# Turning stage one's result of batch 0 on VectorE, with the head of the kernel rearranged

## The chip, the cores and the metric

The kernel runs on one core of a Trainium2 chip. The metric is the device time of one execution in microseconds (us). TensorE is called PE, VectorE DVE, ScalarE ACT, GpSimd POOL and SyncE SP, as in the profile.

## What is computed

For each of 8 batches of 3072 rows by 256 columns, the real part of a two-dimensional Fourier transform; then, row by row, a maxout layer with three weight matrices and an output matrix:

```python
X = np.fft.fft(x, axis=1)
X = np.fft.fft(X, axis=2)
x = X.real.reshape(B * S, D)                 # B, S, D = 8, 3072, 256
h = np.maximum(np.maximum(x @ w1, x @ w2), x @ w3)   # 256 -> 768
out = h @ w_out                                       # 768 -> 256
```

## The kernel before, in words

The transform along the columns is folded into the weights: the matrices `md` and `nmd` hold its sines and cosines, and the products (L290 to L317) of them with w1, w2, w3 give the stationary operands `gE`, `gO` and `gD` of the main loop. The transform along the 3072 rows is split as 32 times 96 and done in two stages per batch.

- **Loading and mirroring.** POOL's queue loads x (L117), and a copy with reversed columns (`mirror`, L124) fills the lower 64 partitions: one copy at L129 and one of a single column at L131. For batch 0 both are on DVE, in four chunks (`FIRST`).
- **Stage one**, `Mix.s` (L365): seven matrix products per batch with the table `tab`; each result in PSUM is evicted to the tile `tb` (L372, L376), with partitions as frequency and the 49 positions s along the row.
- **The turn.** Stage two needs s on the partitions. `Mix.y` (L378) stores `tb` to a DRAM buffer `db` and `Mix.z` (L388) reads it back as `yb`. In batch 0 this is done in six stores and four reads on the queues of SP and ACT. `Mix.u`, `Mix.x0` and `Mix.c` compute one extra column of `yb` from the first column of x.
- **Stage two**, `Mix.k(which, g)` (L406): small products of `yb` with the tables `te_tab` and `to_tab` for one third g of the frequencies; evictions at L413 to `tE` and `tO`, the operands of the main loop. `Mix.end` (L423) does the middle frequency.
- **Tables.** `angle` (L263) reduces the angles in `kvec` with four DVE passes and `table` (L276) makes sines with three ACT passes. Thirds 0 and 1 are done ahead of the loop, the last third (columns 1024 to 1536) by entries of the plan in units 1 to 3.
- **Main loop** (L791 to L829): 18 units per batch, 144 in all. A unit forms two products per 128 hidden columns (`unit_plus`, L430; `unit_minus`, L440), ACT applies relu (`stmp`, L450), DVE takes the maximum into `hp` and `hm` (L451), and the output products (L460) of the previous block are woven in. `third` moves part of odd units to POOL.

The order of the work is written out by hand: engines take instructions in the order of the program, and a plan (L672 to L738) says behind which unit each piece of the next batch's transform is emitted: `ahead0` for batch 1 during batch 0, `ahead` for later ones. `warm_up` (L586) issues products of zeros that keep PE busy while it waits.

Of the head of the program, the order that the prediction follows is at L590 to L637: angles of two thirds on DVE, stage one in three groups with the stores between them, md_all and nmd_all, the first tables, the four reads, the second half of the weights only once a read has landed (L618, L597), four products with 384 columns each, then `m.k(0, 0)` and `m.k(1, 0)`, whose evictions the first unit of the loop waits for.

Of the kernel before, what the change touches and what calls it, by code (L numbers as in the profile page):

```python
# [9 lines left out]
FP32 = mybir.dt.float32  # L10
BF16 = mybir.dt.bfloat16
INT32 = mybir.dt.int32
AX = mybir.ActivationFunctionType
ALU = mybir.AluOpType
# [36 lines left out]
def kernel(  # L51
# [20 lines left out]
    KS = 2 * NS  # L72
# [8 lines left out]
    dbs = [d_pool.tile([NS, 4 * RI * 128], BF16, name=f"db{i}", tag=f"db{i}") for i in range(2)]  # L81
# [5 lines left out]
    tb = consts.tile([128, 25 * 128], BF16, tag="tb")  # L87
    tbv = tb.rearrange("p (s f) -> p s f", f=128)
    yb = consts.tile([128, 2 * RI * 128], BF16, tag="yb")
    x0s = consts.tile([128, RI], BF16, tag="x0s")  # L90
    x0u = consts.tile([128, KS + 1], BF16, tag="x0u")
    ybv = yb.rearrange("p (r e f) -> p r e f", e=2, f=128)
# [13 lines left out]
    gE = [consts.tile([128, DFF], BF16, name=f"gE{i}", tag=f"gE{i}") for i in range(2)]  # L106
    gO = [consts.tile([128, DFF], BF16, name=f"gO{i}", tag=f"gO{i}") for i in range(2)]
    gD = [consts.tile([128, DFF], BF16, name=f"gD{i}", tag=f"gD{i}") for i in range(2)]
# [15 lines left out]
    def mirror(b, s0, s1):  # L124

        t = xt[b % 2]
        fn = (nc.vector.tensor_copy, (nc.gpsimd.tensor_copy, nc.vector.tensor_copy)[s0 >= 25],
              nc.scalar.copy)[min(b, 2)]
        fn(out=t[64:128, s0:s1, 1:128], in_=t[0:64, s0:s1, 255:128:-1])  # L129
        if b < 2:  # L130
            fn(out=t[64:128, s0:s1, 0], in_=t[0:64, s0:s1, 128])  # L131
# [18 lines left out]
    ang_r = gen.tile([128, 4 * RI], FP32, tag="ang_r")  # L150
    iota(ang_r, [[0, 4], [1, RI]], base=1)
    iota(ang_r.rearrange("p (g r) -> p g r", r=RI)[:, :, 15:17], [[0, 4], [16, 2]])
# [9 lines left out]
    def load_w(jh, after=None):  # L162
        for wsrc, wdst in ((moe_w1, w1_bf), (moe_w2, w2_bf), (moe_w3, w3_bf)):
            ld = nc.gpsimd.dma_start(
                out=wdst.rearrange("p (fc j) -> p fc j", fc=2)[:, :, jh * 384:(jh + 1) * 384],
                in_=wsrc.rearrange("(fc p) j -> p fc j", fc=2)[:, :, jh * 384:(jh + 1) * 384])
            if after is not None:
                tc.add_manual_dep(ld.ins, after.ins.name, AFTER, reason="others first")

    load_w(0)  # L170
# [3 lines left out]
    for r in (0, 6, 11):  # L174
        n = {0: 6, 6: 5, 11: 4}[r]
        iota(kv[:, r:r + n, :], [[1, n], [32, 96]], base=r + 1)
    iota(kvec[:, 1408:1504].rearrange("p (r j) -> p r j", r=2), [[16, 2], [32, 48]])
# [3 lines left out]
    rows_f = gen.tile([128, 12 * B], FP32, tag="rows_f")  # L181
    iota(rows_f.rearrange("p (b t u) -> p b t u", t=4, u=3), [[S, B], [-4, 4], [-1025, 3]],
         base=S - 1, cm=-32)
    zero = gen.tile([128, 512], BF16, tag="zero")
    nc.vector.memset(zero, 0.0)
    for db in dbs:
        pads = db[:, 64 * 128:].rearrange("s (r c) -> s r c", c=256)
        nc.sync.dma_start(out=pads, in_=zero[0:NS].rearrange("p (r c) -> p r c", c=256))
# [5 lines left out]
    ang_o = gen.tile([128, 4 * RI], FP32, tag="ang_o")  # L194
    nc.vector.memset(ang_o, 0.0)
    nc.vector.memset(ang_o[:, 0:RI], 8.0)
    nc.vector.memset(ang_o[:, 3 * RI:4 * RI], 24.0)
# [3 lines left out]
    def scal(out, in0, s1, op0, s2=None, op1=None, eng=None):  # L201
# [3 lines left out]

    up, sidx, hflag, alpha, sig, sgm = (small(n) for n in
                                        ("up", "sidx", "hflag", "alpha", "sig", "sgm"))
    scal(up, pidx, 64.0, ALU.is_ge)
    nc.vector.scalar_tensor_tensor(out=sidx, in0=up, scalar=-64.0, in1=pidx,
                                   op0=ALU.mult, op1=ALU.add)  # L210
    scal(hflag, sidx, 32.0, ALU.is_ge)
    scal(alpha, sidx, -2.0, ALU.mult, 31.0, ALU.add)
    nc.vector.scalar_tensor_tensor(out=alpha, in0=alpha, scalar=hflag, in1=sidx,
                                   op0=ALU.mult, op1=ALU.add)
# [3 lines left out]
    ang_q = gen.tile([128, 4 * RI], FP32, tag="ang_q")  # L218
    nc.vector.scalar_tensor_tensor(out=ang_r, in0=ang_r, scalar=alpha, in1=ang_o,
                                   op0=ALU.mult, op1=ALU.add)  # L220
    _reduce(nc, ang_r, ang_r, ang_q, 32.0)
    nc.scalar.activation(out=ang_q, in_=ang_r, func=AX.Sin, scale=float(2.0 * math.pi / 32.0))
    nc.vector.tensor_copy(out=tab[:, 0:64:2], in_=ang_q[:, 0:32])
    scal(tab[:, 1:64:2], ang_q[:, 0:32], sig, ALU.mult)
    scal(tabx, ang_q[:, 2 * RI:4 * RI], sgm, ALU.mult)

    dve = nc.vector.tensor_copy
    half = gen.tile([128, 256], FP32, tag="half")
    nc.vector.memset(half[:, 0:128], 64.0)
    nc.vector.memset(half[:, 128:256], 0.0)  # L230

    vm = gen.tile([128, 512], FP32, tag="vm")
    qm = gen.tile([128, 512], FP32, tag="qm")
    pf = gen.tile([128, 2], FP32, tag="pf")
    par = gen.tile([128, 2], FP32, tag="par")
    for fc in range(2):
# [4 lines left out]
            in1=half.rearrange("p (k c) -> p k c", c=128), op0=ALU.mult, op1=ALU.add)  # L241
    mirror(0, *FIRST[0])
    _reduce(nc, vm, vm, qm, 256.0)
    mirror(0, *FIRST[1])
    mirror(0, *FIRST[2])
    scal(par[:, 1:2], pidx, 0.5, ALU.mult, -0.25, ALU.add)
    scal(par[:, 1:2], par[:, 1:2], ROUND, ALU.add)
    mirror(0, *FIRST[3])
    scal(par[:, 1:2], par[:, 1:2], -ROUND, ALU.add, -2.0, ALU.mult)
    nc.vector.tensor_tensor(out=par[:, 1:2], in0=par[:, 1:2], in1=pidx, op=ALU.add)  # L250
    scal(par[:, 1:2], par[:, 1:2], 64.0, ALU.mult)
    scal(par[:, 0:1], par[:, 1:2], -1.0, ALU.mult, 64.0, ALU.add)
    nc.vector.tensor_copy(out=vm.rearrange("p (fc k c) -> p fc k c", fc=2, k=2)[:, :, :, 0],
                          in_=par.unsqueeze(1).to_broadcast([128, 2, 2]))
    phi, s_of = small("phi"), small("s_of")
    scal(phi, par[:, 1:2], 12.0, ALU.mult, 768.0, ALU.add)
    scal(s_of, par[:, 1:2], -1.0 / 64.0, ALU.mult)
    nc.vector.tensor_tensor(out=s_of, in0=s_of, in1=pidx, op=ALU.add)
    scal(s_of, s_of, 0.5, ALU.mult)
    q = gen.tile([128, NHALF + 1], FP32, tag="q")  # L260
    step = float(2.0 * math.pi / 3072.0)

    def angle(part, c0=1024, c1=NHALF + 1):  # L263
        cs = slice(c0, c1)
        if part == 0:
            scal(kvec[:, cs], kvec[:, cs], s_of, ALU.mult, phi, ALU.add)
# [4 lines left out]

    def angles(c0, c1):
        for part in range(2):
            angle(part, c0, c1)
# [11 lines left out]
    def tables(c0, c1):  # L286
        for k in range(3):
            table(k, c0, c1)

    def product(i, half, jh, pool, tag):  # L290

        psg = pool.tile([128, 512], FP32, name="psg", tag=tag)
        hs = slice(half * 128, (half + 1) * 128)
        for k, (table, wt) in enumerate(((md, (w2_bf, w3_bf)[i]), (nmd, w1_bf))):
            for fc in range(2):
                nc.tensor.matmul(
                    psg[:, 0:384], table[fc][:, hs],
                    wt[:, fc * DFF + jh * 384: fc * DFF + jh * 384 + 384],
                    start=(k == 0 and fc == 0), stop=(k == 1 and fc == 1))
        return psg  # L300

    def keep_product(psg, i, half, jh, evict_e):

        cs = slice(jh * 384, (jh + 1) * 384)
        if half == 0:
            evict_e(out=gE[i][:, cs], in_=psg[:, 0:384])
        else:
            nc.scalar.copy(out=gO[i][:, cs], in_=psg[:, 0:384])
            nc.vector.tensor_scalar(out=gD[i][:, cs], in0=gO[i][:, cs], scalar1=dif,
                                    scalar2=None, op0=ALU.mult)  # L310
# [551 lines left out]
```

## Time and profile before

| what | us |
|---|---|
| runs shown | 400.01, 401.09, 401.16 (median 401.09) |
| the profiled execution's own time | 400.15 |
| its span, first to last instruction | 397.9 |
| PE busy | 382.8 (96%) |
| DVE busy | 317.6 (80%) |
| ACT busy | 259.6 (65%) |
| POOL busy | 324.6 (82%) |
| granted PE clock, mean | 0.989 of full |

The page of the profile shows the execution in 40 slices of 9.9 us; a digit is the busy share of an engine in tenths:

```
PE   7598999999999999999999999999999999999994
DVE  6977797877887887877887877887887887887982
ACT  2577689768856788568866788568766547544420
PEclk9799999999999999999999999999999999999999
```

PE is below nine tenths only in the first four slices and the last. The second slice, 10 to 20 us, is where PE is busy half the time and has a lower clock; all that the prediction works out lies there and in the two slices behind it.

### The profile page before, as it was taken

To read this page: it belongs to the slowest core of one execution; us is meant where nothing else is said; L and a number is where in the kernel's file an instruction comes from. 1 tells how busy PE (TensorE), PEld (TensorE's weight loads), DVE (VectorE), ACT (ScalarE), POOL (GpSimd) and SP (SyncE) were. 2 spreads that over 40 slices of the span, in tenths; PEclk is the share of its full clock that TensorE was granted. 3 is DMA by queue.
4 is the path that set the end of the run, shared out by engine and by line. 5 is a ranking of instruction groups with operands and counts; after the bars stand their busy time and mean duration, and the time that the engine had idled before them with its cause. 6 is when DMAs were issued, how large, how long until landed. Compare 5 with 4: busy or idle time off the path is not lost.

```text
span 397.9 us, 8345 instructions
## 1 busy us (share of the span) xinstructions
PE 382.8 (96%) x2739; PEld 236.3 (59%) x2739; DVE 317.6 (80%) x542; ACT 259.6 (65%) x466; POOL 324.6 (82%) x408
## 2 busy tenths in 40 slices
PE   7598999999999999999999999999999999999994
PEld 2254466656665666666665666666665666666673
DVE  6977797877887887877887887877887887887982
ACT  2577689768856788568866788568766547544420
POOL 7376389879988899889988899889878798879993
PEclk9799999999999999999999999999999999999999
DMA  8989987494776777395776877394432563322234
GB/s 121 196 175 195 167 229 147 122 192 145 141 154 123 177 165 162 108 190 148 147 155 117 183 166 153 108 200 127 129 112 82 133 154 104 91 77 50 88 88 138
DMA packets 69532, 56.30 MB, mean 141 GB/s; under 512 B 35040, under 2 KB 64992, under 8 KB 68292
## 3 DMA queue, kind: packets, MB, share of 16 engines
q0 software_dynamic: 23552, 26.53, 35.9%
q1 hardware_dynamic: 44898, 28.70, 28.1%
q10 hardware_dynamic: 1040, 0.56, 0.5%
q8 instruction: 21, 0.34, 0.4%
q14 instruction: 21, 0.17, 0.1%
HBM read 38.15 MB, written 31.71 MB: 176 GB/s over the span
## 4 chain that ended last, share of the span: by engine, by line
PE 86%; DMA 6%; ACT 3%; DVE 2%; POOL 1%; issue 1%; SPq 0%; POOLq 0%; DVEq 0%; ACTq 0%
PE po L460 30%; PE pse L444 11%; PE pse L436 7%; PE pse L437 7%; PE po L483 5%; PE pse L772 4%; PE pse L773 4%; PE e L756 4%; PE d L758 4%; PE ps L369 3%; DMA yb<-db 3%; PE ps L411 3%; PE pl L475 2%; DMA xt<-in_x_dram 2%; ACT stmp L450 1%; POOL xt L122 1%
## 5 line engine op out<-in xcount | busy, mean ns | idle before, releaser
L450 ACT ACTIVATE stmp<-pse 128x512 bf16<-128x512 f32 x150 | 89.6, 600 | 64.0 <-PE pse L444 39.8
L570 POOL DMA_INDIRECT out_dram<-ot,rows_m x92 | 102.3, 1112 | 17.9 <-issue 7.5
L765 POOL TENSOR_TENSOR plus<-even,odd 128x512 bf16<-128x512 f32 x69 | 87.9, 1274 | 34.0 <-DVE even L761 26.9
L765 POOL TENSOR_TENSOR minus<-even,odd 128x512 bf16<-128x512 f32 x69 | 87.6, 1270 | 0.0
L460 PE MATMUL po<-wout_bf,hp 128*128 128x256 bf16 x576 | 86.1, 273 | 0.0
L774 DVE SCALAR_TENSOR_TENSOR hp<-pse,plus 128x512 bf16<-128x512 f32 x69 | 47.6, 689 | 46.7 <-PE pse L773 26.2
L460 PE MATMUL po<-wout_bf,hm 128*128 128x256 bf16 x576 | 78.6, 273 | 0.0
L460 PEld LDWEIGHTS <-hp 128*128 128x128 bf16 x576 | 56.4, 98 | 26.1
L444 PE MATMUL pse<-tO,gD 128*128 128x512 bf16 x219 | 70.9, 379 | 0.0
L460 PEld LDWEIGHTS <-hm 128*128 128x128 bf16 x576 | 56.4, 98 | 16.3
L488 DVE TENSOR_TENSOR ot<-po,even 128x512 f32<-128x512 f32 x92 | 62.6, 681 | 0.0
L451 DVE TENSOR_TENSOR hp<-pse,stmp 128x512 bf16<-128x512 f32 x75 | 51.4, 685 | 10.8 <-ACT stmp L450 9.4
L436 PE MATMUL pse<-tE,gE 128*128 128x512 bf16 x150 | 56.8, 378 | 2.0 <-DVE hm L451 0.7
L451 DVE TENSOR_TENSOR hm<-pse,stmp 128x512 bf16<-128x512 f32 x75 | 51.5, 687 | 7.1 <-ACT stmp L450 3.9
L437 PE MATMUL pse<-tO,gO 128*128 128x512 bf16 x150 | 56.8, 379 | 0.0
L761 DVE SCALAR_TENSOR_TENSOR even<-vb,wcol,e 128x512 f32<-128x512 bf16 x69 | 50.8, 737 | 0.0
L786 DVE SCALAR_TENSOR_TENSOR hm<-pse,minus 128x512 bf16<-128x512 f32 x69 | 47.0, 681 | 0.9 <-PE pse L437 0.3
L760 ACT ACTIVATE odd<-d 128x512 f32<-128x512 f32 x69 | 41.3, 598 | 6.6 <-POOL minus L765 0.4
L129 ACT COPY xt<-xt 64x762 bf16<-64x762 bf16 (+1 forms) x48 | 40.2, 838 | 1.1
L372 ACT CAST tb<-ps 128x512 bf16<-128x512 f32 x46 | 24.8, 589 | 21.5 <-PE ps L369 21.5
L444 PEld LDWEIGHTS <-gD 128*128 128x128 bf16 x219 | 21.4, 98 | 23.1 <-issue 5.0
L483 PE MATMUL po<-gw,tO 128*128 128x512 bf16 x92 | 34.9, 380 | 0.0
(156 smaller groups left out, 468.3 us busy)
## 6 DMA issues: line engine op xcount, KB each, us to landing
yb<-db SPq DMA_DIRECT2D x7, 833.0 KB
xt<-in_x_dram POOLq DMA_DIRECT2D x14, 384.0 KB, 9.2
out_dram<-ot SPq DMA_DIRECT2D x55, 96.0 KB
out_dram<-ot SPq DMA_DIRECT2D x64, 64.0 KB
db<-tb SPq DMA_DIRECT2D x21, 192.0 KB
vb<-vd SPq DMA_DIRECT2D x23, 128.0 KB
xt<-in_x_dram POOLq DMA_DIRECT2D x7, 400.0 KB, 7.3
xt<-in_x_dram POOLq DMA_DIRECT2D x7, 368.0 KB
```

The costliest lines, as they stand in the source:

```text
L436: nc.tensor.matmul(pse[:, 0:n], gE[i][:, js], te, start=True, stop=False)
L437: nc.tensor.matmul(pse[:, 0:n], gO[i][:, js], to, start=False, stop=True)
L444: nc.tensor.matmul(pse, gD[i][:, js], to, start=False, stop=True, skip_group_check=True)
L450: nc.scalar.activation(out=stmp[:, 0:n], in_=pses[0][:, 0:n], func=AX.Relu)
L451: nc.vector.tensor_tensor(out=dst, in0=src3, in1=stmp[:, 0:n], op=ALU.max)
L460: nc.tensor.matmul(po, hcols(jc), wout_bf[:, jc * 256:(jc + 1) * 256], start=False, stop=(jc == NJC - 1), skip_group_check=True)
L483: nc.tensor.matmul(po, to[:, cp], gw[:, 256:768], start=True, stop=True)
L488: nc.vector.tensor_tensor(out=ot.rearrange("p (h c) -> p h c", h=2), in0=po.rearrange("p (h c) -> p h c", h=2), in1=lin.unsqueeze(1).to_br ...
L570: stored(nc.gpsimd.indirect_dma_start(out, bass.IndirectOffsetOnAxis(ap=rows_m[0:128 - lo, at_row: at_row + 1], axis=0), ot[lo:128, 256:51 ...
L761: nc.vector.scalar_tensor_tensor(out=even3, in0=vb, scalar=wcol[:, jc:jc + 1], in1=e3, op0=ALU.mult, op1=ALU.add)
L765: nc.gpsimd.tensor_tensor(out=dst, in0=even3, in1=odd3, op=op)
L774: nc.vector.scalar_tensor_tensor(out=dst, in0=pse2, scalar=0.0, in1=sums[g][0], op0=ALU.max, op1=ALU.max)
```

## The change

Stage one's result of batch 0 no longer goes through DRAM. `tb` becomes a tile of 32-bit words, each with two neighbouring columns of bf16; stage one's evictions of batch 0 write it with the 32 positions s innermost, and one DVE instruction (`Mix.t`) transposes each block of 32 partitions by 32 words into `yb`. Rows of `yb` are renumbered: all 128 partitions are used, even and odd s in two halves of 64, and slots are shifted by one (`Mix.col`). `Mix.f` fills the slots at the edge with two ACT copies and four memsets.

```diff
+    tb = consts.tile([128, 64 * 32], UINT32, tag="tb")
+    tbw = tb.rearrange("p (f s) -> p f s", s=32)
+    tbt = tb.bitcast(BF16).rearrange("p (f s l) -> p f s l", s=32, l=2)
+    yb = consts.tile([128, 2 * RI * 64], UINT32, tag="yb")
+    ybw = yb.rearrange("p (q f) -> p q f", f=64)
...
-                evict(out=tb[:, k * 512:(k + 1) * 512], in_=ps1)
+                if self.b:
+                    evict(out=tbv[:, 4 * k:4 * k + 4, :],
+                          in_=ps1.rearrange("p (s f) -> p s f", s=4))
+                else:
+                    evict(out=tbt[:, :, 4 * k:4 * k + 4, :],
+                          in_=ps1.rearrange("p (s f l) -> p f s l", s=4, l=2))
...
+        def t(self):
+            nc.vector.transpose(out=ybw[:, 2:34, :].rearrange("p q f -> p f q"), in_=tbw)
+
+        def f(self):
+            for a in (0, 64):
+                nc.scalar.copy(out=ybv[a + 32:a + 64, 0], in_=ybv[a:a + 32, 16])
+                for r in (0, 32):
+                    nc.vector.memset(ybw[a:a + 32, r:r + 2, :], 0)
```

Later batches still go through DRAM, with four reads in two calls in place of one, and `x0` writes its column into `yb` directly, later in the plan, in place of `c`:

```diff
-        def z(self, i0=0, i1=RI, s0=0, s1=NS):
-            rows = self.db.rearrange("s (c q) -> (s c) q", c=2)
-            return nc.sync.dma_start(out=yb[2 * s0:2 * s1, i0 * 256:i1 * 256],
-                                     in_=rows[2 * s0:2 * s1, i0 * 256:i1 * 256])
+        def z(self, hh):
+            n = 25 - hh
+            for (p0, q0, q1, at) in ((0, 0, 30, 2), (32, 30, 64, 0)):
+                nc.sync.dma_start(
+                    out=ybz[64 * hh + p0:64 * hh + p0 + n, at * 128:(at + q1 - q0) * 128],
+                    in_=self.db[hh::2, q0 * 128:q1 * 128])
...
-              8: ("z",), 9: ("x",), 12: ("c",), 13: ("kO0",), 14: ("v0", "kE0", "kO1"),
+              8: ("z0", "z1"), 12: ("x",), 13: ("kO0",), 14: ("v0", "kE0", "kO1"),
...
-    ahead = {1: ("s0", "s1"), 2: ("s2", "y0", "s3", "s6"), 3: ("s4", "s5", "y1", "u"), 5: ("x",),
-             7: ("z",), 11: ("c",), 12: ("kO0",), 13: ("v0", "kE0", "kO1"), 14: ("v1", "kE1"),
+    ahead = {1: ("s0", "s1"), 2: ("s2", "y0", "s3", "s6"), 3: ("s4", "s5", "y1", "u"),
+             6: ("z0",), 7: ("z1",), 11: ("x",), 12: ("kO0",), 13: ("v0", "kE0", "kO1"),
```

The head of DVE and ACT is put in another order. Two of the passes of each angle reduction go to ACT (`turns`) and one stays on DVE (`mad`, a multiply and add in one instruction; `wrap` for kvec); `par` comes ahead of `tab`; the single columns of batch 0's first three chunks go to ACT. The weights are loaded in nine pieces, the last three no longer behind the reads, and the products are formed in pieces of 128, 256 and 384 columns, evicted into one tile `g_all` (for gE and gO) and one `gd_all` (for gD, by `differ`).

```diff
+    scal(par[:, 1:2], pidx, 0.5, ALU.mult, -0.25, ALU.add)
...
+    nc.vector.tensor_copy(out=tab[:, 0:64:2], in_=ang_q[:, 0:32])
...
+    def turns(q, v, per):
+        nc.scalar.activation(out=q, in_=v, func=AX.Identity, scale=1.0 / per, bias=rnd[:, 0:1])
+        nc.scalar.activation(out=q, in_=q, func=AX.Identity, scale=1.0, bias=rnd[:, 1:2])
+
+    turns(qm, vm, 256.0)
...
     mirror(0, *FIRST[0])
...
+    phase(0, 512)
+    turns(q[:, 0:512], kvec[:, 0:512], 3072.0)
+    mad(vm, qm, -256.0, vm)
...
+    nc.vector.memset(tbw[:, :, 24:32], 0)
+    mirror(0, *FIRST[1])
...
     m.s(1, pool=ps_s)
-    m.y(0, 16)
     warm_up(5)
+    wrap(0, 512)
+    mirror(0, *FIRST[2])
+    nc.scalar.activation(out=md_all, in_=vm, func=AX.Sin, scale=float(2.0 * math.pi / 256.0))
     m.s(2, pool=ps_s)
     m.s(3, pool=ps_s)
-    m.y(16, 32)
+    phase(512, 1024)
+    mirror(0, *FIRST[3])
     m.s(4, pool=ps_s)
-    m.s(5, pool=ps_s)
+    scal(sgn, pidx, 0.0, ALU.is_equal)
+    scal(sgn, sgn, 2.0, ALU.mult, -1.0, ALU.add)
+    m.s(5, pool=ps_s, evict=dve)
     m.s(6, pool=ps_s)
-    m.y(32, NS, nc.scalar)
+    m.t()
     nc.scalar.activation(out=nmd_all, in_=vm, func=AX.Sin, scale=float(-2.0 * math.pi / 256.0))
+    table(0, 0, 512)
+    table(1, 0, 512)
+    table(2, 0, 512)
+    for k in range(3):
+        load_w(k, 384, 768)
     m.u()
-    m.z(0, 6, 0, 32)
-    m.z(0, 6, 48, NS)
-    landed = m.z(0, 6, 32, 48)
-    m.z(6, RI)
-    load_w(1, landed)
+    scal(qs, kvec[:, 512:1024], 1.0 / 3072.0, ALU.mult, ROUND, ALU.add, eng=nc.gpsimd)
+    scal(qs, qs, -ROUND, ALU.add, eng=nc.gpsimd)
...
+    psg0 = products(ps_f, 0, 2, 0, 128)
+    keep(psg0, 0, 2, 0, 128, nc.scalar.copy)
+    psg1 = products(ps_s, 0, 1, 128, 384)
+    m.x0(x0s)
+    warm_up(2)
+    m.c(1, 7)
+    m.k(0, 0, dve)
+    m.k(1, 0)
+    psg2 = products(ps_s, 1, 2, 128, 384)
+    wrap(512, 1024)
+    keep(psg1, 0, 1, 128, 384, dve)
+    scal(dif, sgn, 1.0, ALU.subtract)
+    differ(0, 2, 0, 128)
+    keep(psg2, 1, 2, 128, 384, dve)
     table(1, 512, 1024)
+    rows_f = gen.tile([128, 12 * B], FP32, tag="rows_f")
+    iota(rows_f.rearrange("p (b t u) -> p b t u", t=4, u=3), [[S, B], [-4, 4], [-1025, 3]],
+         base=S - 1, cm=-32)
...
-    for (u, fn) in ((0, lambda: next(second)), (0, lambda: m.c(6, RI, nc.scalar.copy)),
+    for (u, fn) in ((0, lambda: table(2, 512, 1024)), (0, lambda: m.c(7, 16)),
+                    (0, lambda: next(second)), (0, lambda: differ(0, 2, 128, 384)),
+                    (1, lambda: table(0, 512, 1024)), (2, m.f), (2, lambda: m.c(0, 1)),
+                    (2, lambda: m.c(16, RI)),
                     (1, lambda: m.k(1, 1)), (1, lambda: next(second)), (1, lambda: angle(0)),
```

More of the change, by code (lines that the diff above doesn't have):

```diff
@@ L284, in table, with product @@
                                  bias=half_pi)
[L286 to L292, printed above, removed]
+    def product(psg, c, i, half, j0, j1):
         hs = slice(half * 128, (half + 1) * 128)
```

262 lines of the change are left out of this document (128 added, 134 removed).

## The prediction

> **What bounds it now.** I read the page first: PE is busy 96% of 397.9 us, and 86% of the chain that ended last is PE. By the waits of PE over the whole span it is held up only in the head, apart from 0.4 us, so what reaches the end is the time at which the head lets PE run full. The chain of work, in order of time, names the head:
>
> ```profile
> 5.71 7.38 DMA xt<-in_x_dram
> 15.46 3.71 DMA db<-tb
> 19.52 2.63 DMA yb<-db
> ```
>
> Stage one's result goes to DRAM and back: 15.46 to 22.15, the piece that the change replaces. Next the timelines of PE and DVE (start, length, what, and in brackets the idle time before it and its releaser):
>
> ```profile
> 16.74 0.82 PE L296 MATMUL psg<-w_bf,md_all 128*128 128x384 bf16 x2 [1.72 <-ACT md_all L609]
> ...
> 21.34 0.59 PE L588 MATMUL warm<-zero 128*128 128x512 bf16 x2
> 22.28 0.39 PE L411 MATMUL ps<-te_tab,yb 98*128 98x96 bf16 x6 [0.34 <-DMA yb<-db]
> ...
> 23.45 0.38 PE L436 MATMUL pse<-tE,gE 128*128 128x512 bf16 x1 [0.53 <-DVE tE L413]
> ```
>
> ```profile
> 22.71 0.69 DVE L413 CAST tE<-ps 128x512 bf16<-128x512 f32 x1 [1.28 <-PE ps L411]
> 23.32 0.31 DVE L309 TENSOR_SCALAR gD<-gO,dif 128x384 bf16<-128x384 bf16 x1
> 24.71 0.69 DVE L451 TENSOR_TENSOR hp<-pse,stmp 128x512 bf16<-128x512 f32 x1 [1.08 <-ACT stmp L450]
> ...
> 32.53 0.32 DVE L309 TENSOR_SCALAR gD<-gO,dif 128x384 bf16<-128x384 bf16 x1 [0.43 <-ACT gO L308]
> ...
> 33.22 0.69 DVE L270 TENSOR_TENSOR kvec<-kvec,q 128x513 f32<-128x513 f32 x1
> ```
>
> Two things to see. While the round trip runs, PE computes products until 21.3 and waits for the read only 0.34 us: the trip is mostly covered. And from 22.71 to 33.91 DVE is idle only 1.5 us; its L270 there (the angles of the last third of the tables) releases ACT's tables at 34.0 and with them the end of batch 0's head. I call its end **K = 33.91** and ask when K comes after the change. Last, the stretches of 1 us (length, busy time of PE, PEld, DVE, ACT, POOL, then the granted PE clock):
>
> ```profile
> 17.00:18.00 1.00, 1.00 (x5) 0.41 (x3) 0.97 (x2) 0.46 (x3) 0.00 (x0) 0.50 1.22 268
> ...
> 20.00:21.00 1.00, 1.00 (x5) 0.47 (x4) 0.96 (x5) 1.00 (x3) 0.00 (x0) 0.59 0.78 207
> 21.00:22.00 1.00, 0.94 (x6) 0.29 (x3) 0.42 (x1) 0.59 (x2) 0.00 (x0) 1.00 0.60 151
> ```
>
> From 14.0 to about 20.8 PE has half its clock: the products pass at 0.32 us per 384 columns, 0.83 ns a column; behind it two of them take 0.32.
>
> **The change, part by part.**
>
> *DVE ahead of the transposition.* Removed: three of batch 0's four column copies (L131), now ACT's, and two of three passes of each angle reduction, now ACT's. Added: one memset of 512 words (L154: 0.27 for 256, so 0.54). Moved: par's six operations ahead of tab, 0.18 each. Step by step from the old rows: the reduction for tab ends at 4.75, half 0.22, par 1.1, tab 0.45, vm 1.28, rnd 0.1, phi and s_of 0.55: the first mirror at 8.5 (7.84 before). Mirror 0.61, phase 0.58, vm 0.72, par's copy 0.17, memset 0.54, mirror 0.73, wrap 0.72, mirror 0.6, phase 0.57, mirror and column 0.8: 14.5, against 13.96. PE's s(5) then ends at 15.2 and its eviction, now on DVE (0.69), at 15.9. ACT gets four Identity passes (L283, with a bias: 0.72), three columns (0.25) and the early md_all; from 9.75 these and its evictions sum to 5.8 us, so s(6) is out at 15.7 and nmd_all at 16.3.
>
> *Evictions into the turned layout.* Runs of 16 bytes instead of one row. No row shows it. Below: 0.59 (L372); above: ACT's row with one element per 512 bytes, 4.5 ns each, 2.3 us. A run has eight elements, so the contiguous row is nearer: 0.59.
>
> *The transposition:* 2048 words per partition, written 256 bytes apart. No transposition is in the trace. The nearest rows are strided copies:
>
> ```profile
> L136 ACT COPY xt<-xt 64x49 bf16<-64x49 bf16 x6 | 2.5, 409 | 0.1
> L404 ACT COPY yb<-x0s 98x17 bf16<-98x17 bf16 x7 | 1.9, 265 | 1.1 <-DMA yb<-db 1.0
> L131 DVE COPY xt<-xt 64x12 bf16<-64x12 bf16 x2 | 0.4, 184 | 0.0
> L131 DVE COPY xt<-xt 64x9 bf16<-64x9 bf16 x1 | 0.2, 164 | 0.0
> ```
>
> ACT: (409-265)/32 = 4.5 ns an element. DVE's own, over the 155 ns that its contiguous copies leave after their elements: 1.0 ns (9 elements) and 2.4 ns (12). Bounds: 1.0 ns, 2.2 us, and ACT's 4.5 ns, 9.4 us with the fixed part. I take the middle of DVE's two, 1.7 ns: 3.6 us, 15.95 to 19.6.
>
> [...]
>
> *PE up to the first k.* Products in the order 128, 256, then 256 columns, the last behind k. From nmd_all at 16.3: 14 products of 128 columns at 0.83 ns, 1.5; eight of 256, 1.7; x0 0.15, two warm matmuls 0.85: k(0,0) at 20.5, its result at 21.1. The transposition (19.6) is hidden by them by 0.9 us; without that cover each us counts. c(1,7) on ACT comes at 20.4. So tE's eviction starts at 21.1 (22.71 before): **1.6 us won**.
>
> *DVE from there to K.* Behind tE's eviction stand, in order, wrap 0.72, two product evictions 0.61 each, dif 0.1, differ 0.25 (L309: 0.31 for 384), all ahead of the first hp; later differ 0.4 and m.f's four memsets 0.5. Old busy time to K: 11.2 - 1.5 idle = 9.7. New: 9.7 - 0.3 (gD) + 2.3 + 0.9 = 12.6. K = 21.1 + 12.6 = 33.7 plus 0 to 0.4 idle: **33.9, nothing won**. The wait for DRAM goes, DVE's queue is late next. ACT gets two copies for m.f (about 0.28) and two small columns in units 0 to 2, where it is idle over 2 of 4 us from 28 to 32. With idle 0 to 0.4 the part is worth from a gain of 0.2 to a loss of 0.2.
>
> *DMA and POOL.* The weights come in six pieces and the second half no longer waits 8.1 us for yb; POOL's in-order queue then issues batch 1's loads about 6 us sooner, which nothing waits for. The two q operations on POOL (0.6 to 1.3 each, between its copy and its tensor operation of 512) end by 19, ahead of wrap. The row numbers' iota (0.79) goes behind these loads. u() grows by one copy, 0.2 per batch, on an engine that PE doesn't wait for here.
>
> *Later batches.* x0 now writes yb itself: two ACT copies for two. One read of 98 rows becomes two of 25 and two of 24, 0.35 each on SP's queue. The trace's completion events: a read of 98 rows gives 15, the first at 0.5 us, 49 rows 8, 2 rows 3; one more than the largest divisor up to 16. So 25 rows would go by 5 engines. A packet of 8704 bytes passes in about 0.39 us; five engines get 10 + 4 of them instead of 7. Batch 1: 53.2 + 2.0 for the first + 13 x 0.39 + 0.5 = 60.8, and ACT needs it at 60.72; later batches issue the first pair one unit (2.4 us) sooner, which pays for it. I take 0.1; bounds 0 and 1.5.
>
> The sum: 0 + 0.1 on the profiled execution's own 400.15 (span 397.9): 400.25. The runs shown have a median of 401.09; the four times average 400.6, so I say **400.7**.
>
> **Rivals.**
>
> *The clock holds.* If PE has its full clock from 16.3, the products take 1.6, warm 0.43, k(0,0) comes at 18.6. With DVE's lower price the transposition ends at 18.2; tE starts at 18.9, K at 31.7: -2.2, 398.0. Where: the products between 16.3 and 20.5. For it: the clock came back at 20.8 behind 4 us of unbroken products, so when it moves hangs on where gaps and bursts fall, and these move. Against: it fell at 14.0 behind 7 us in which PE was busy 59%, and by the steps above the same 7 us have 58% after.
>
> *Strided writes cost DVE what they cost ACT.* 9.4 us: transposition to 25.3, tE at 25.9, K at 38.5: +4.6, 404.8, slower. It decides from 4.6 us on, where the products no longer cover it. For it: ACT's rows agree over 17 and 49 elements; against: DVE's own rows.
>
> *The reads on five engines come late.* In one batch (275.18) a read took 8.63 instead of 5.8 and ACT stood 1.0 us. At that ratio, 1.5, batch 1's would be late by 3 us and six others by up to 1; PE's queue hides perhaps half: +2, 402.3. [...]
>
> **The numbers.** Forecast 0.42, clock 0.28, strided writes 0.18, reads 0.12. A measurement of this kernel tells 0.3% (1.2 us) from no change. Faster: the clock's 0.28 and 0.07 of the forecast's edge; slower: 0.18, half of the reads and 0.03: 0.27; the rest, 0.38, is the same. The range goes from the clock's 398.0 to 403.4, which leaves out the upper part of the strided writes; the forecast's own is 400.0 to 401.6.
>
> **What would show it.** The transposition's length, 2.2 to 9.4 us, and its end against 20.5; the clock between 14 and 21; tE's eviction at 21.1; five DVE operations between it and the first hp; K near 33.9; the read of batch 1 against ACT's x0 copy. A K before 33 or after 35 makes the prediction wrong.

## The result

The changed kernel takes 403.33 us (median of 6 executions, 402.58 to 403.71), the kernel before 401.12 (6 executions). The ratio is 1.0058, 95% interval 1.0042 to 1.0074: slower by 0.6%. The profiled execution took 403.34, its span is 401.5. It lies 3.2 us above the profiled one of before, and the medians 2.2, because the profiled execution of before (400.15) lies 1.0 below that kernel's median. The forecast was 400.7, no change, with K at 33.9.

The chain of work of the kernel after, in order of time (start, length, what). It answers the three DMA lines of before: no DMA is left between stage one and stage two.

```profile
15.88 3.38 PE psg L314 x22
19.30 0.87 PE warm L640 x2
20.17 0.44 PE ps L466 x6
20.63 0.69 DVE tE L468
```

The timeline of DVE from there to K, the end of the last angle operation (L297 now):

```profile
15.73 3.75 DVE L434 STREAM_TRANSPOSE yb<-tb 128x2048 uint32<-128x2048 uint32 x1
20.63 0.69 DVE L468 CAST tE<-ps 128x512 bf16<-128x512 f32 x1 [1.15 <-PE ps L466]
...
22.89 0.68 DVE L328 CAST g_all<-psg 128x512 bf16<-128x512 f32 x1
24.89 0.69 DVE L504 TENSOR_TENSOR hp<-pse,stmp 128x512 bf16<-128x512 f32 x1 [1.31 <-ACT stmp L503]
...
26.09 1.45 DVE L335 TENSOR_SCALAR gd_all<-g_all,dif 128x512 bf16<-128x512 bf16 x1
...
31.41 0.68 DVE L440 MEMSET yb<- 32x128 uint32 x4
...
33.21 0.35 DVE L335 TENSOR_SCALAR gd_all<-g_all,dif 128x384 bf16<-128x384 bf16 x1 [0.54 <-ACT g_all L344]
...
35.17 0.35 DVE L335 TENSOR_SCALAR gd_all<-g_all,dif 128x384 bf16<-128x384 bf16 x1 [0.55 <-ACT g_all L344]
...
35.89 0.69 DVE L297 TENSOR_TENSOR kvec<-kvec,q 128x513 f32<-128x513 f32 x1
```

The transposition takes 3.75 us and tE's eviction comes 2.1 us earlier than before (22.71). Yet K = 35.89 + 0.69 = 36.58, 2.67 later than 33.91. Between the two points DVE needs 15.95 us, against 11.2 before and 12.8 in the forecast. This distance, **from tE to K**, is the measure for what follows: a few tenths by which a whole head comes earlier or later in one execution drop out of it. Of the 15.95 us DVE is busy for 13.28 and idle for 2.67; before, it was busy for 9.60 and idle for 1.60; the forecast had 12.6 of work "plus 0 to 0.4 idle".

PE, POOL and ACT in the same stretch, one fence each (in brackets the idle time ahead of the line and what ended it):

```profile
23.63 0.38 PE L490 MATMUL pse<-tE,g_all 128*128 128x512 bf16 x1 [1.71 <-DVE g_all L328]
...
28.79 0.38 PE L490 MATMUL pse<-tE,g_all 128*128 128x512 bf16 x1 [1.30 <-DVE hm L504]
```

```profile
25.83 1.56 POOL L134 COPY xt<-xt 64x1651 bf16<-64x1651 bf16 x1
27.33 0.30 POOL L138 COPY xt<-xt 64x13 bf16<-64x13 bf16 x1
27.54 1.45 POOL L134 COPY xt<-xt 64x1524 bf16<-64x1524 bf16 x1
```

```profile
30.25 0.83 ACT L438 COPY yb<-yb 32x256 bf16<-32x256 bf16 x2
32.03 0.29 ACT L459 COPY yb<-x0s 128x1 bf16<-128x1 bf16 x2 [0.95 <-DVE yb L440]
32.22 0.58 ACT L468 CAST tE<-ps 128x512 bf16<-128x512 f32 x1
```

POOL's first copy starts at 25.83, DVE's differ (the 1.45 us above) at 26.09: they run beside each other, and differ ends at 27.54, just behind the copy (27.39). Before the change the same copy ran behind K, since its loads were issued later (at 24.59 and 26.66; after the change, at 18.71 and 20.87):

```profile
34.29 1.56 POOL L129 COPY xt<-xt 64x1651 bf16<-64x1651 bf16 x1 [3.04 <-DMA xt<-in_x_dram]
```

The first hp of each unit, after less before, is where the time is lost in order: +0.18 in unit 0, +1.45 in unit 1, +2.67 in unit 3, +2.6 up to unit 13 of batch 0, then +3.4 from unit 16. The second step is batch 1's reads: ACT waits for them at the copy of the extra column, where it did not wait before.

```profile
64.61 0.23 ACT L455 CAST yb<-psx 128x16 bf16<-128x16 f32 x1 [1.38 <-DMA yb<-db]
```

Later batches add 0.3 and give 0.3 back, and the last hp is 3.4 later than before.

### The profile page after: what moved, and what is told of

The parts are those of the page before. It is cut to its first block, busy times and chain, and to the rows that moved or that the text cites. A ratio compares the mean times of both kernels' runs of the same rounds, so it can differ in the third digit from the quotient of the medians.

```text
span 401.5 us, 8422 instructions
## 1 busy us (share of the span) xinstructions
PE 383.7 (96%) x2755; PEld 237.7 (59%) x2755; DVE 321.0 (80%) x542; ACT 262.6 (65%) x476; POOL 329.9 (82%) x422
## 4 chain that ended last, share of the span: by engine, by line
PE 89%; DVE 5%; ACT 3%; issue 1%; DVEq 0%; ACTq 0%
PE po L513 31%; PE pse L497 12%; PE pse L490 8%; PE pse L491 8%; PE po L536 5%; PE pse L830 4%; PE pse L831 4%; PE e L814 4%; PE d L816 4%; PE ps L401 3%; PE ps L466 3%; PE pl L528 2%; PE psg L314 1%; ACT stmp L503 1%; DVE hp L504 1%
## 5 line engine op out<-in xcount | busy, mean ns | idle before, releaser
L497 PE MATMUL pse<-tO,gd_all 128*128 128x512 bf16 x219 | 70.8, 379 | 0.0
L490 PE MATMUL pse<-tE,g_all 128*128 128x512 bf16 x150 | 56.8, 379 | 4.5 <-DVE hm L504 2.1
L491 PE MATMUL pse<-tO,g_all 128*128 128x512 bf16 x150 | 56.8, 379 | 0.0
L497 PEld LDWEIGHTS <-gd_all 128*128 128x128 bf16 x219 | 21.3, 97 | 23.1 <-issue 5.0
L405 ACT CAST tb<-ps 128x512 bf16<-128x512 f32 x40 | 21.6, 588 | 14.8 <-PE ps L401 14.0
```

The source lines that it names most:

```text
L490: nc.tensor.matmul(pse[:, 0:n], g_all[:, jc, 2 * i, :], te, start=True, stop=False)
L491: nc.tensor.matmul(pse[:, 0:n], g_all[:, jc, 2 * i + 1, :], to, start=False, stop=True)
L497: nc.tensor.matmul(pse, gd_all[:, jc, i, :], to, start=False, stop=True, skip_group_check=True)
```

## The experiments

Each is an edit of the changed kernel unless said otherwise. Times are from profiled executions; the ratio is against executions of the kernel before that were measured beside that run, with its 95% interval.

| run | tE to K | K | hp, unit 4 | ratio |
|---|---|---|---|---|
| before | 11.20 | 33.91 | 36.43 | 1 |
| after | 15.95 | 36.58 | 39.04 | 1.0058 (1.0042 to 1.0074) |
| e1_mirror_later | 16.64 | 36.61 | 39.70 | 1.0066 (1.0042 to 1.0090) |
| e2_keep_on_act | 16.43 | 36.51 | 38.97 | 1.0077 (1.0052 to 1.0103) |
| e3_f_unit3 | 14.13 | 34.03 | 38.02 | 1.0048 (1.0026 to 1.0071) |
| e4_three | 13.16 | 33.16 | 36.94 | 1.0028 (1.0006 to 1.0051) |
| e5_hold | 14.86 | 34.82 | 37.28 | 1.0037 (1.0025 to 1.0050) |
| e15_hold_f | 13.59 | 33.47 | 35.93 | 1.0001 (0.9976 to 1.0025) |
| e6_head | 12.97 | 33.22 | 35.69 | 0.9975 (0.9963 to 0.9987) |
| e13_spread_first | 12.79 | 32.67 | 35.14 | 0.9961 (0.9936 to 0.9986) |

**GpSimd's copies beside DVE.** e1 lets the first copy wait for differ:

```diff
+        if b == 1 and s0 == 0:
+            tc.add_manual_dep(cp.ins, held[0].ins.name, AFTER, reason="differ first")
```

> The changed kernel, with one edit: GpSimd's first mirror copy for batch 1 (64x1651) waits until VectorE's differ of 128x512 in unit 0 is done. Theory 'the two engines collide': differ took 1.45 us because this copy, now 7 us earlier than before the change, ran beside it; without the copy it takes 0.40, hp of unit 1 comes at 26.4 instead of 27.46, K at about 35.5 instead of 36.58, and the end is 1.0 us earlier than the changed kernel (ratio to the kernel before near 1.003). Rival 'its own layout': differ reads and writes runs of 128 elements out of a larger tile and takes 1.45 by itself; then it stays at 1.4 and no time moves. Rival 'given back': differ shrinks and K does not move, because something else in units 1 and 2 is late next.

DVE of this run:

```profile
25.43 0.34 DVE L337 TENSOR_SCALAR gd_all<-g_all,dif 128x512 bf16<-128x512 bf16 x1
...
27.49 0.54 DVE L215 TENSOR_SCALAR kvec<-kvec,s_of,phi 128x513 f32<-128x513 f32 x1
28.07 1.56 DVE L215 TENSOR_SCALAR q<-kvec 128x513 f32<-128x513 f32 x1
```

Differ is 0.34, so its layout is not the cause. But the angle operation q, 0.43 in the changed kernel, now takes 1.56: the collision moved, and K stayed. e5 holds both copies until K (the same lines, with the last angle operation in place of differ):

> The changed kernel, with GpSimd's two mirror copies for batch 1 held until K (the last angle operation of DVE), where they also stood before the change. In the earlier runs the collision only moved: where differ escaped it, the angle operation q of 128x513 took 1.56 to 1.67 us instead of 0.43. Theory 'the copies cost DVE 1.1 to 1.2 us wherever they fall before K': now neither operation is long, hp of unit 2 comes 1.1 us earlier than in a run with the collision, and K with it if DVE's queue sets K (35.4). Rival 'ACT's queue sets K': ACT's column waits for f's memsets, the tE and product evictions stand behind it, and so K moves by less than 0.5 although hp of unit 2 is 1.1 earlier.

```profile
25.42 0.36 DVE L337 TENSOR_SCALAR gd_all<-g_all,dif 128x512 bf16<-128x512 bf16 x1
...
28.06 0.43 DVE L215 TENSOR_SCALAR q<-kvec 128x513 f32<-128x513 f32 x1
```

Neither is long now, and tE to K falls from 15.95 to 14.86, by 1.1: so much the collision cost in the changed kernel's execution, where it hit one operation. Where a head comes a little earlier, it can hit two: in e9 and e11 below, which have the changed kernel's head, the two angle operations took 1.04 and 1.70, and 1.31 and 1.70, and tE to K was 17.9 and 18.3. That is 3.1 to 3.4 more than with the hold. The longer operations make up 1.8 to 2.0 of it. The rest, 1.3 to 1.4, is PE's clock. It shows in the products that follow in unit 2, one group for g1t and four pairs with 384 columns (the first two lines of e9, then of e5, where nothing collides):

```profile
32.77 1.01 PE L370 MATMUL pst<-md_all,w_bf 128*128 128x256 bf16 x4 [3.17 <-DVE g_all L344]
33.57 0.84 PE L314 MATMUL psg<-w_bf,md_all 128*128 128x384 bf16 x2
```

```profile
30.97 0.60 PE L372 MATMUL pst<-md_all,w_bf 128*128 128x256 bf16 x4 [1.39 <-DVE g_all L346]
31.40 0.49 PE L316 MATMUL psg<-w_bf,md_all 128*128 128x384 bf16 x2
```

In e9 PE stands for 3.17 us behind the operations that were hit, the granted clock falls from 1.00 to 0.50 at 32.0, and these products take 3.2 us instead of 1.9. The same happened in e11 (idle 3.43, 3.3 us), in e2 below (2.63, 3.25) and in part in e1 (2.52, 2.55), where 0.65 of clock and 1.13 of q give the 1.78 between 16.64 and 14.86. In the changed kernel itself PE stood for only 1.39 us there, and in e7 for 2.38, and the clock stayed at 1.00.

**The first unit and f.** e2 puts the evictions of the second and third group of products on ACT:

```diff
-    keep(psg1, 0, 1, 128, 384, dve)
+    keep(psg1, 0, 1, 128, 384, nc.scalar.copy)
...
-    keep(psg2, 1, 2, 128, 384, dve)
+    keep(psg2, 1, 2, 128, 384, nc.scalar.copy)
```

> The changed kernel, with the evictions of the second and third group of products on ACT instead of DVE. Theory 'the first unit waits for DVE's queue through a PSUM bank': its first matmul writes the bank that the third group of products leaves, and that eviction stood fifth on DVE (22.89 to 23.57). On ACT it ends at about 22.6, so the first unit's matmul starts at 22.7 instead of 23.63 and the first hp at 24.0 instead of 24.89. As differ then ends before GpSimd's copy at 25.83, it should take 0.4 too, and the end is 1.5 to 2.0 us earlier than the changed kernel (ratio near 1.001). Rival 'ACT is no better': ACT has tO's eviction and the table passes in the same 2 us; the first hp moves by less than 0.3 and the end by less than 0.5.

DVE first, then ACT:

```profile
23.31 0.69 DVE L504 TENSOR_TENSOR hp<-pse,stmp 128x512 bf16<-128x512 f32 x1 [1.49 <-ACT stmp L503]
...
27.15 1.67 DVE L213 TENSOR_SCALAR q<-kvec 128x513 f32<-128x513 f32 x1
```

```profile
30.60 0.29 ACT L459 COPY yb<-x0s 128x1 bf16<-128x1 bf16 x2 [2.19 <-DVE yb L440]
```

The first hp comes 1.58 earlier, 1.03 of it counted from tE; 0.9 was expected of the wait on the PSUM bank. The end does not come earlier. What was won is lost in unit 2: q collides (1.24 longer), ACT stands 2.19 us (0.95 in the changed kernel) for f's memsets, with the evictions of tE and of the products behind it, and the clock falls (1.35). Against e5 that is 1.24 + 1.35 - 1.03 = 1.56, and 16.43 - 14.86 = 1.57 was measured. e3 moves f and the two small columns to the end of unit 3:

```diff
-                    (2, m.f), (2, lambda: m.c(0, 1)), (2, lambda: m.c(16, RI)),
+                    (3, m.f), (3, lambda: m.c(0, 1)), (3, lambda: m.c(16, RI)),
```

> The changed kernel, with f (two copies of ACT, four memsets of DVE) and the two small columns moved from unit 2 to the end of unit 3, since nothing reads them ahead of unit 4. Theory 'they stand on DVE's way to K': DVE loses 0.68 us of memsets, and ACT's column no longer waits 0.95 us for them, so that the product evictions come sooner and DVE's two waits of 0.54 shrink; K at 35.6 instead of 36.58, the end 0.9 to 1.2 us earlier than the changed kernel (ratio near 1.003). Rival 'moved, not saved': the same work in units 3 and 4 delays the last third's evictions, and the end moves by less than 0.3.

K falls to 34.03, by 2.5 (1.8 of it between tE and K), more than expected. But the hp of unit 4 gains only 1.0, since in unit 3 ACT has the three table passes, f and the evictions in one row:

```profile
35.36 0.62 ACT L302 ACTIVATE te_tab<-kvec 128x513 bf16<-128x513 f32 x1
35.99 0.83 ACT L438 COPY yb<-yb 32x256 bf16<-32x256 bf16 x2
36.96 0.54 ACT L459 COPY yb<-x0s 128x1 bf16<-128x1 bf16 x2
37.40 1.08 ACT L503 ACTIVATE stmp<-pse 128x512 bf16<-128x512 f32 x2
```

From K to the hp of unit 4 this run needs 3.99, the kernel before 2.52. K alone was too short a yardstick. e4 has the three edits at once:

> The three edits together. Theory 'the head's loss is these three': K near 33.5 to 34.0 (33.91 before the change, 36.58 after it), and the end 2.7 to 3.1 us earlier than the changed kernel; what is left against the kernel before is batch 1's and 2's later reads, 0.8 to 1.0 us, so a ratio of 1.000 to 1.002 by the profiled runs and a little below by the medians. Rival 'one of them is only hidden by another': the sum is clearly less than the three taken singly.

K = 33.16, earlier than expected, and unit 4 again late (3.78 behind K), so that the ratio is 1.0028 where 1.000 to 1.002 was expected. q is again hit (1.67). f costs in unit 2 and in unit 3, so the next run puts it into a gap. e6 has the hold of e5, the evictions of e2, and f whole on DVE ahead of the first hp:

```diff
+    m.f()
...
-                nc.scalar.copy(out=ybv[a + 32:a + 64, 0], in_=ybv[a:a + 32, 16])
+                nc.vector.tensor_copy(out=ybv[a + 32:a + 64, 0], in_=ybv[a:a + 32, 16])
...
-                    (2, m.f), (2, lambda: m.c(0, 1)), (2, lambda: m.c(16, RI)),
+                    (0, lambda: m.c(0, 1)), (0, lambda: m.c(16, RI)),
```

> The hold of the mirror copies, the two product evictions on ACT, and f whole on DVE in its gap ahead of the first hp (22 to 23.2 in the runs with the evictions on ACT), the two small columns on ACT in unit 0. Theory 'the change's own gain is there, and what eats it in the head is the collision, the eviction ahead of the first unit and f's place': first hp near 23.3, no DVE operation of unit 0 to 2 above 0.75, K at 31.0 to 32.0 (33.91 before), hp of unit 4 at 34.3 to 35.3 (36.43 before), the end 0.3 to 1.0 below the kernel before, with batch 1's later reads (0.7) still in it: ratio 0.996 to 1.000. Rival 'ACT is full': with the table passes and evictions ACT has no 2 us left between 20 and 35, and hp of unit 4 does not come before 36.4.

The first hp is at 23.89 and that of unit 4 at 35.69, 0.74 earlier than before the change. K is 33.22, not 31 to 32. The ratio is 0.9975: **faster than both kernels**. DVE's gap holds f, though one copy ran beside GpSimd's row numbers (0.83 where the other took 0.22; that the one caused the other was not tried):

```profile
22.03 0.22 DVE L440 COPY yb<-yb 32x256 bf16<-32x256 bf16 x1
22.33 0.30 DVE L442 MEMSET yb<- 32x128 uint32 x2
22.65 0.83 DVE L440 COPY yb<-yb 32x256 bf16<-32x256 bf16 x1
23.55 0.30 DVE L442 MEMSET yb<- 32x128 uint32 x2
23.89 0.69 DVE L506 TENSOR_TENSOR hp<-pse,stmp 128x512 bf16<-128x512 f32 x1
```

e15 leaves the evictions on DVE, with the hold and with f ahead of the first hp:

> The changed kernel with the mirror copies held and f on DVE ahead of the first hp, but with the two product evictions on DVE, as the change has them. The hold alone gave K = 34.82, hold, f and evictions together 33.22. Theory 'f's place and ACT's wait for its memsets are the larger part': K at 33.2 to 33.8. Rival 'the first unit's wait on the PSUM bank is': K at 34.3 to 34.8.

tE to K is 13.59, as the first theory said. So the steps are: hold 1.09 (15.95 to 14.86), f 1.27 (to 13.59), evictions 0.6 to 0.8 (to 12.97 in e6, 12.79 in e13). By DVE's busy and idle time they are of different kinds:

| from tE to K | length | busy | idle |
|---|---|---|---|
| after | 15.95 | 13.28 | 2.67 |
| e5, hold | 14.86 | 12.18 | 2.68 |
| e15, hold and f | 13.59 | 12.55 | 1.04 |
| e6, hold, f and evictions | 12.97 | 11.95 | 1.02 |

The hold takes off busy time, the new place of f takes off idle time, and the evictions take off busy time again, since they leave DVE for ACT. Once f fills DVE's gap ahead of the first hp, the wait on the PSUM bank costs DVE nothing more.

**Later batches' reads.** e7 splits each read into 16 rows and the rest:

```diff
+                for (r0, r1) in ((0, 16), (16, n)):
```

> The changed kernel, with each of the four reads per batch split into 16 rows and the rest (9 or 8), so that all 16 engines take part; eight issues instead of four. Theory 'five engines carry the 25-row reads': an engine then has at most 8 packets of a batch instead of 14, the last row of batch 1 lands near 62.5 instead of 64.38, ACT's wait of 1.38 us at the x0 copies of batch 1 goes, and the growth of the lag from unit 13 to unit 16 of batch 0 (0.8 us) shrinks to 0.2 or less; the end 0.5 to 0.9 earlier than the changed kernel. Rival 'the issues': each issue costs SP 0.35, the last read is issued 1.4 later, and the landing stays within 0.5 of 64.4. Rival 'shared rings': stores and other loads fill the 16 engines in that stretch, so more engines do not help; landing unchanged too, but with the stores later.

It made things worse: the lag grows by 1.4 from unit 13 to 16, not 0.8. The rows themselves are through at 63.81 (64.04 in the changed kernel), yet ACT goes on only at 65.39; what holds up the last completion is not shown. e9 splits the 25-row reads by parity instead, into every second partition:

```diff
+                for (r, st) in (((0, 2), (1, 2)) if n == 25 else ((0, 1),)):
```

> The changed kernel, with each read of 25 rows split by parity: 13 rows into every second partition and 12 into the others; the 24-row reads stay. Six issues per batch instead of four. With 16 rows side by side per read, all engines took part and the packets only took longer (7680 bytes: 0.42 us before that edit, 0.67 after it), so the bytes per second stayed. Theory 'both counts matter, the engines of a read and how far apart the partitions lie that they write at one time': 13 and 12 engines writing every second row of 25 partitions: packets near 0.5, the rows of batch 1 through in about 5.5 us instead of 7.5, landed near 62.5 instead of 64.38, and the lag does not grow between units 13 and 16 by more than 0.3 (0.8 in the changed kernel). Rival 'four or more reads in line are slow whatever their shape': each read's rows follow the read ahead on the same engines; the stretch stays at 7.0 us or more and the lag grows by 0.8 to 1.4 again.

Here the lag does not grow at all, and ACT no longer waits for the DMA. From the trace's DMA records, batch 1's rows (engines by completion events):

```
run      rows of a read, engines          first to last row   mean row   rate
before   98 on 14                         4.37 us             0.50 us    195 GB/s
after    25 on 5, 24 on 12                7.54                0.47       106
e7       16 on 16, 9 on 9, 8 on 8         7.03                0.80       114
e9       13 on 13, 12 on 12, 24 on 12     5.45                0.44       147
```

With 16, 9 and 8 engines on as many neighbouring partitions (e7) a row takes 1.7 times as long (0.80 us against 0.47) and the rate stays nearly the same (114 against 106 GB/s); with 13 and 12 engines on every second partition (e9) it rises to 147. (In e9 the rows that are read lie twice as far apart in DRAM too; which side matters was not separated.) What slows the neighbouring rows is not shown. The landing itself was not at 62.5 but at 64.8: this run's head was 1.3 later, and SP went from one of the split reads to the next in 0.8 us, not 0.35. The ratio of e9, 1.0138 (1.0108 to 1.0168), goes with its head, in which two operations collided and the clock fell: its last hp is 4.4 later than before, 3.9 of it already at unit 13.

e8 joins e6 and e7:

> The head's edits and the reads on 16 engines together. If both theories hold: hp of unit 4 at 34.3 to 35.3, no growth in batch 1's stage above 0.2, and the end 1.0 to 2.0 us below the kernel before (ratio 0.995 to 0.998). If the reads do not help by themselves: as the run with the head's edits alone.

Unit 4's hp at 35.32, then 1.5 us of growth in batch 1; ratio 0.9991 (0.9975 to 1.0007). e10 joins e6 and e9:

> The head's edits (ratio 0.9975 by themselves) with the reads split by parity. If the spread reads land in time: no growth in batch 1's stage, the end 0.6 to 0.8 below the head's edits alone: ratio 0.995 to 0.997. If not: 0.997 to 0.999.

No growth in batch 1 (1.34 ahead of the kernel before), but in batches 3 and 4 two stalls of 0.6 and 0.8 at unit 12, part of it recovered; ratio 0.9989 (0.9971 to 1.0008). So e13 splits batch 1 alone (`n == 25 and self.b == 1`):

> The head's edits, with the reads split by parity for batch 1 alone; batches 2 to 7 keep their four reads. With all batches split, batch 1's stage lost nothing (lag unchanged from unit 13 to 16), but two later batches stalled by 0.6 and 0.8. Theory 'the extra issues are late only where the reads are issued in two units under the stores': the gain of batch 1 stays (about 1.3 us below the kernel before in batch 1) and no stall follows; the end 1.2 to 1.8 below the kernel before, ratio 0.9955 to 0.997. Rival: the stalls come anyway, ratio 0.997 to 0.999.

399.13 us against 400.62: 0.9961 (0.9936 to 0.9986). The lead of 1.3 is kept to the last hp, and by its median it is **the fastest version here**, though its interval overlaps that of e6 (0.9963 to 0.9987). That batch 1's stage gains is shown: the lag grows by 0.0 in e9, e10 and e13, by 0.8 in the changed kernel and in e6. That the extra issues under the stores made the stalls of e10 was not tried by itself.

**The transposition itself.** e11 writes its result contiguously (batch 0 then has its rows in another order):

```diff
-            nc.vector.transpose(out=ybw[:, 2:34, :].rearrange("p q f -> p f q"), in_=tbw)
+            nc.vector.transpose(out=yb[:, 128:2176].rearrange("p (f q) -> p f q", q=32), in_=tbw)
```

> The changed kernel, with the transposition writing its 2048 words per partition side by side instead of 256 bytes apart, so that batch 0's rows stand in another order than the later steps read them: batch 0's result is not the reference's. It prices the layout. Theory 'the spread writes set its 3.75 us' (1.75 ns a word, as forecast from the strided copies): contiguous it takes 2.2 us or less (1.0 ns a word). Theory 'the transposition has its own rate': it stays at 3.7. In both, the end moves by less than 0.5 us, since what follows it in the head, not its end, sets K; in a run in which PE keeps its full clock the first k could start up to 1.0 earlier.

```profile
15.78 2.31 DVE L434 STREAM_TRANSPOSE yb<-tb 128x2048 uint32<-128x2048 uint32 x1
19.76 0.69 DVE L468 CAST tE<-ps 128x512 bf16<-128x512 f32 x1 [1.66 <-PE ps L466]
```

2.31 against 3.75: the spread writes cost 1.4 us, and 2.3 are the transposition's own, so neither theory is right as it stands. Hidden as they are behind the products, they hardly move tE: 19.76, against 19.9 to 20.3 in the runs with 3.75 (20.6 in the changed kernel, whose granted clock was 0.50 to 0.52 from 18 to 21 and 1.00 from 21 to 22, and 20.9 in e7). Its ratio, 1.0091 (1.0069 to 1.0113), goes again with the collision and the clock behind it.

e12 and e14 are e6 with batch 0 sent through DRAM as the later batches are: its evictions write rows again, two further stores stand ahead of those shown, f is left out, and one memset clears `yb` ahead of the reads:

```diff
-    m.t()
+    m.y(24, NS)
+    nc.vector.memset(yb, 0)
+    m.z(0)
+    m.z(1)
```

> The kernel with the head's edits, but batch 0 goes through DRAM again, written and read as the later batches are, with the rest of the new head kept; f is left out, and yb is cleared once in place of the transposition. It prices the transposition alone in a head that does not waste it. The trip was 15.46 to 22.15 before the change, and by four reads on five engines no shorter: the first k at 22.5 to 23.5 instead of 20.3, the first hp 2 to 3 us later than 23.9. Theory 'the transposition's gain reaches the end once the queue behind it is cleared': hp of unit 4 is 1.5 to 3.0 us later than 35.69, and the end 1.5 to 3.0 later (ratio 1.001 to 1.005). Rival 'the rest of the head sets K anyway': hp of unit 4 at most 0.7 later.

The trip took from 14.0 to 35.0, ratio 1.0421 (1.0401 to 1.0441). Neither theory had this: the second half of the weights and batch 1's loads, which the change issues early (here between 14.21 and 22.52), went through the DMA engines with it. e14 holds them until the reads have landed, as the kernel before does:

> Batch 0 through DRAM again in the head with the edits, but with the second half of the weights and batch 1's loads held until the reads have landed, as the kernel before holds them. Without the hold the trip took from 14.0 to 35.0, since those loads lay ahead of it in the DMA queues. Theory 'the transposition buys freedom from the loads, and little more than the trip's uncovered part': held, the reads land between 22.5 and 25.5, the first hp at 25.5 to 28.5 (23.9 with the transposition), and the end is 1.5 to 4.5 us later than with it (ratio 1.001 to 1.009). Rival 'the trip itself is long in this head': four reads take as long as before the hold, landing after 30, ratio above 1.02.

```profile
19.05 0.38 PE L641 MATMUL warm<-zero 128*128 128x512 bf16 x1
27.23 0.58 PE L467 MATMUL ps<-te_tab,yb 128*128 128x96 bf16 x6 [7.80 <-DMA yb<-db]
```

The reads land at 27.1, between the two forecasts, and the end is about 8.9 us behind e6 (medians 408.51 and 399.62, not measured side by side; ratio 1.0185, 1.0143 to 1.0228). With nothing but the end of the stores beside them the four reads still took from 19.1 to 27.1, where before the last piece that k waited for landed at 22.15. So in the new layout and head the transposition is worth nearly nine microseconds, because its own DRAM trip would be so slow: 7.6 of them are there at tE (27.85 against 20.25), and 1.1 more come up to K; behind its wait of 7.8 us PE runs at half its rate (from 31.00 to 32.28 it starts a product of 512 columns every 0.43 us, from 32.76 on every 0.22). Against the old trip, mostly covered, it won 2.1 us at tE.

## Why the prediction was wrong

**Right.** The round trip was mostly covered; the transposition (3.75 measured, 3.6 forecast) is hidden by the products, and tE's eviction comes at 20.6 (21.1 forecast). DVE's queue is late next. The 3.6 was in part luck: it took the middle of 1.0 and 2.4 ns a word from two strided copies, but e11 shows 2.31 us for the transposition without a stride and 1.44 for the stride. The stride makes it 1.6 times as long.

**The clock.** In the profiled execution it fell and came back at about 21 (0.52 from 14 to 18, 0.50 from 18 to 20, 1.00 from 21 to 22), as the forecast assumed. The rival's gain of 2.2 does not come where its condition holds: in e2 and e5 the granted clock was 1.00 from 14 to 22, and tE came at 20.08 and 19.96, 0.6 to 0.7 earlier than 20.63, because there the transposition (15.84 + 3.74 in e2) becomes the bound. The rival's 18.9 needed a transposition of 2.2 us.

**Wrong: "DVE from there to K"**, 12.8 us forecast, 15.95 measured. The step that failed is "plus 0 to 0.4 idle": DVE was idle for 2.67 us. The prediction itself read 1.5 us of idle there in the kernel before, and took them out without a reason. The largest parts of the 2.67 are 1.31 ahead of the first hp and two waits of 0.54 and 0.55 for ACT's product evictions. Idle time is 2.5 of the 3.15 us that were missing. The other 0.7 is busy time, 13.28 against 12.6: there the collision added 1.1, and the other terms came out 0.4 lower than forecast. The runs give three causes.

1. "POOL's in-order queue then issues batch 1's loads about 6 us sooner, which nothing waits for". Nothing waits for the loads, but GpSimd's copies wait on them, and these moved from 34.29 to 25.83, into DVE's busiest stretch: an earlier transfer was priced by who waits for it, not by what it sets going. "Differ 0.4" became 1.45, and e5, which holds the copies, gives 1.09 back. What the two engines hold each other up by is not shown. The operations that grew read and write SBUF: differ from 0.34 (e1) to 1.45 (after), q from 0.43 (e5) to 1.56 (e1) and 1.70 (e9, e11), the one ahead of q from 0.53 (e5) to 1.04 (e9) and 1.31 (e11). Those from PSUM beside the same copies stayed at 0.68 (after: hp and hm at 27.46 and 28.06, beside the copy from 27.54 to 28.99).
2. "m.f's four memsets 0.5", and "two copies (about 0.28)" on ACT "where it is idle". The memsets took 0.68, the copies 0.83, and between them stands a wait across the engines: ACT's small column waits for the memsets, the product evictions stand behind it on ACT, DVE waits for these twice. With f in the gap ahead of the first hp (e15), the 0.68 leave DVE's way and one of the two waits (0.55) is gone: 1.23 of the 1.27 that were measured. Only the sum of durations was counted, not who stands behind whom.
3. The forecast listed the two product evictions "ahead of the first hp" by their 0.61 us. It missed that the first unit's matmul writes the PSUM bank that the last of them empties: PE stood 1.71 us for it, and with the evictions on ACT (e2) the first hp came 1.03 earlier, counted from tE. The 0.6 to 0.8 of the last step (e15 to e6 and e13) is not this wait, which f already filled, but the work that leaves DVE.

The three steps sum to 3.0 to 3.2, and the forecast was short by 3.15. That these agree is in part chance: the last step takes work off DVE that the forecast had counted.

**Mis-sized: the reads.** "I take 0.1; bounds 0 and 1.5": measured 0.8 in batch 1. The engine count was right (5 and 12), the time of a row nearly so (0.39 taken, 0.42 to 0.53 measured); but the stretch took 7.5 us, not the 13 x 0.39 = 5.1 of the sum. The sum's start, 53.2, stands in no row: before, this read was issued at 53.93. Its 2.0 for the first row was 0.9. The rival that gave +2 named the right place, but five engines are not the whole cause: 16, 9 and 8 (e7) did not help (114 GB/s against 106).

The sum by measured terms: +2.6 (head) + 0.8 (reads) + 0.3 - 0.3 = 3.4, which is the lag of the last hp in the profiled pair; the two times differ by 3.2, the spans by 3.6.

What stays open: how much of the collision falls into one execution. One to two operations were hit, worth 1.1 to 2.0 us by themselves and up to 3.4 with the clock behind them, in executions whose heads differ by some tenths.

## What to carry to other kernels

A sum of work on one engine needs a line for its waits: take over the idle time of the kernel before unless you can say why it goes. When an edit lets a transfer start sooner, follow it through to the compute that it releases, and ask which engine that will run beside. Before pricing an operation in an in-order queue by its length, list what stands behind its waits on every engine, and which PSUM bank the next stage takes over. Test a suspected collision by holding the other side well past the stretch: in e1, moving it by one instruction only moved the loss.

## What the runs showed of the hardware

- DVE's transposition of 2048 words per partition: 2.31 us with contiguous writes (e11), 3.75 with writes 256 bytes apart (after).
- Rows of 7680 and 8704 bytes into SBUF: reads on 16, 9 and 8 engines on as many neighbouring partitions moved hardly more (114 GB/s, e7) than 5 and 12 engines on 25 and 24 (106, after); 13 and 12 engines on every second partition, beside 12 on 24 neighbours, moved 147 (e9), one read of 98 rows of 8704 bytes on 14 engines 195 (before).
- An issue on SP that writes every second partition was followed by the next 0.8 to 0.9 us later (e9), one of neighbouring rows 0.35 to 0.45 later (e7).
- In unit 2, where PE stood idle for 2.5 to 3.4 us (e1, e2, e9, e11), the granted clock fell to 0.50 during or behind it, and the products that follow took 2.55 (e1) to 3.3 us, against 1.9 in e5; where PE stood for 1.39 (after, e5) or 2.38 (e7), it stayed at 1.00.
